# Small per-row operations moved to two-tensor VectorE forms, and the conversion of w2 staged over two steps

## The chip, the cores and the metric

The kernel runs on one core of a Trainium2 chip. The metric is the device time of one execution in microseconds; several executions are taken and the median is given. A profile of one further execution gives the trace from which durations are read. TensorE does the matrix products, VectorE (DVE in the profile), ScalarE (ACT) and GpSimd (POOL) do the elementwise work, and SyncE (SP) only issues DMAs.

## What is computed

```python
# q, k, v: (8, 8, 576, 64); tau = 0.02
scores = scale * np.matmul(q, k.transpose(0, 1, 3, 2))
thresh = np.max(scores, axis=-1, keepdims=True) - tau
scores = np.where(scores >= thresh, scores, -1000000000.0)
scores = scores - np.max(scores, axis=-1, keepdims=True)
attn = np.exp(scores)
attn = attn / (np.sum(attn, axis=-1, keepdims=True) + 1e-09)
x = np.matmul(attn, v)                    # heads side by side: (8, 576, 512)
...
mixed = np.real(np.fft.fft(np.fft.fft(x, axis=1), axis=2))
u = x + mixed
un = (u - mean(u)) / np.sqrt(var(u) + 1e-06)      # per row of 512
ch = np.maximum(un @ w_ch1, 0.0) @ w_ch2          # 512 -> 2048 -> 512
out = u + ch
```

Everything that the reference calls single precision is fp32 in the kernel. The weights w_ch1 and w_ch2 come as 64-bit floats, of which the kernel makes fp32 itself.

## The kernel before, in words

The eight batches have eight heads each, taken in pairs: 4 pairs a batch, 32 pairs in all. A pair has 5 row tiles (t = 0 to 4): four of 128 query rows for two heads, and a last one in which the 64 remaining rows of both heads share the 128 partitions. So there are 160 steps, i = 5 n + t.

A step's `scores(i)` makes the score rows in PSUM (L394, L405 for t = 4), takes each row's negated maximum on VectorE (`neg`, L416), makes the threshold of the row from it (`thr`, L420), takes the exponential on ScalarE (L426), and masks it on VectorE (L429), which also yields the row's sum `den`. A constant is added to the sum (L433), its reciprocal is taken (L436), and GpSimd copies it over 128 columns into `rec` (L438), because TensorE is to transpose it. For t = 4 GpSimd also copies 64 columns of the exponentials (L442). `transposed_weights(i - 1)`, one step later, turns exponentials and `rec` round on TensorE (L468, L469, L482) and ScalarE copies them out of PSUM. After a pair's five steps `weighted_values` makes v times the weights for both halves of the rows (L503), and VectorE multiplies each half by the turned reciprocals (`x`, L508). `fold_rows`, mostly on GpSimd (L531 to L544), and `mixing` make the Fourier part; its sums go to `u_t`, a ring of two batches' columns. `channels` then runs the two layers in groups of 384 rows: L685 for the first, L706 for the second.

The weights: `convert` turns one chunk of 64-bit floats into fp32 as a generator that stops between stages: a mask on VectorE (L283), a ScalarE scaling (L287), two VectorE operations (L289, L294), two ScalarE ones (L299, L303), and two GpSimd multiplies (L305, L306). There are 16 chunks of w_ch1 with stages in buffers of their own (loaded over SP's queue), and 16 of w_ch2, whose raw bits lie in the yet unused second half of `u_t`: two chunks' room, and loads on GpSimd's queue (L276). Matmuls that read `u_t` in the first half of the ring are ordered behind the conversion's writes, the last of which is L303. `center` takes the column mean from w_ch1, a group of 512 columns at a time; each has four subtractions (`less_mean`, L349), two on VectorE and two on GpSimd.

The order. Steps 0 to 19 (the first batch) are ordered wholly by hand: `step(i)` emits the scores, then one of the weighted values, a piece of centring (`later`), or two dummy matmuls that keep TensorE busy (`busy(2)`); then stages of two w_ch1 chunks around the previous step's transposed weights, then whatever centring has put into `after`. From step 20 on only TensorE's order is by hand; a scheduler orders the other engines. In each step there, `fill()` (three times) emits Fourier work and one or more matmul groups of `channels` within a budget. For the first sixteen steps from 21 on, one w_ch2 chunk is converted as a whole behind the step's reciprocal (`issue_after`, which fixes the order of issue on that engine alone), and the chunk two further on is then fetched:

```python
for _ in chunks.pop(0):
    pass
j = i - per_batch + 1
if j < NJ:
    chunks.append(w2_chunk(j))
```

Of the kernel before, what the change touches and what calls it, by code (L numbers as in the profile page):

```python
# [47 lines left out]
def kernel(  # L48
# [12 lines left out]
    nc = tc.nc  # L61
# [40 lines left out]
    def busy(n):  # L102

        for _ in range(n):
            pd = ps.tile([128, 4, 128], FP32, tag="mm", bufs=4, name="pd")
            four = bass.AP(
                tensor=ones.tensor, offset=ones.offset, ap=[list(ones.ap[0]), [0, 4], [1, 128]]
            )
            nc.tensor.matmul(pd[:, :, :], ones[:, :], four, start=True, stop=True)
# [76 lines left out]
    nc.vector.tensor_scalar(  # L186
        out=tau_pos[:], in0=tau_t[:], scalar1=0.0, scalar2=-1.0, op0=ALU.max, op1=ALU.mult
    )
    thr_off = const.tile([128, 1], FP32, name="thr_off")
    nc.vector.tensor_tensor(out=thr_off[:], in0=tau_pos[:], in1=below[:], op=ALU.add)  # L190

# [187 lines left out]
        if n + 1 < B * NPAIR:  # L381
            load_pair(n + 1)

    def scores(i):
        n, t = divmod(i, NT)
        qT, kT = heads[n][0:2]

        nh = 2 if t < 4 else 1
        sc = [ps.tile([128, 2, 512], FP32, tag="sc", name=f"sc{j}") for j in range(nh)]
        if t < 4:  # L390
            for c in range(2):
                for j in range(2):
                    hp = slice(64 * j, 64 * j + 64)
                    nc.tensor.matmul(  # L394
                        sc[j][:, c, 0:HALF], qT[hp, 128 * t : 128 * t + 128],
                        kT[hp, HALF * c : HALF * (c + 1)], start=True, stop=True,
                    )
        else:

            for j, c, c0, k0, w in (  # L400
                (0, 0, 0, 0, HALF), (1, 0, 0, 64, HALF), (0, 1, 0, HALF, HALF),
                (1, 1, 0, 64 + HALF, 512 - HALF), (1, 1, 512 - HALF, 0, 64),
            ):
                hp = slice(64 * j, 64 * j + 64)
                nc.tensor.matmul(  # L405
                    sc[0][hp, c, c0 : c0 + w], qT[hp, 512:S], kT[hp, k0 : k0 + w],
                    start=True, stop=True, skip_group_check=True,
                )
        neg = sb.tile([128, 2], FP32, tag="neg", bufs=3, name="neg")
        thr = sb.tile([128, 2], FP32, tag="thr", bufs=3, name="thr")  # L410
        den = sb.tile([128, 2], FP32, tag="den", bufs=3, name="den")


        e = sb.tile([128, 2 * S], FP32, tag="e", name="e")
        for j in range(nh):
            nc.vector.tensor_reduce(  # L416
                out=neg[:, j : j + 1], in_=sc[j][:, :, 0:HALF], axis=AXIS_XY, op=ALU.max,
                negate=True,
            )
        nc.vector.tensor_scalar(  # L420
            out=thr[:, 0:nh], in0=neg[:, 0:nh], scalar1=-1.0, scalar2=thr_off[:, :],
            op0=ALU.mult, op1=ALU.add,
        )
        for j in range(nh):
            ej = e[:, S * j : S * (j + 1)].rearrange("p (c n) -> p c n", c=2)
            nc.scalar.activation(  # L426
                out=ej, in_=sc[j][:, :, 0:HALF], func=ACT.Exp, bias=neg[:, j : j + 1], scale=1.0
            )
            nc.vector.scalar_tensor_tensor(  # L429
                out=ej, in0=sc[j][:, :, 0:HALF], scalar=thr[:, j : j + 1], in1=ej,  # L430
                op0=ALU.is_ge, op1=ALU.mult, accum_out=den[:, j : j + 1],
            )
        nc.vector.tensor_scalar(  # L433
            out=den[:, 0:nh], in0=den[:, 0:nh], scalar1=1e-9, scalar2=None, op0=ALU.add
        )
        behind[0] = nc.vector.reciprocal(den[:, 0:nh], den[:, 0:nh])  # L436
        rec = sb.tile([128, 2 * D], FP32, tag="rec", name="rec")
        nc.gpsimd.tensor_copy(  # L438
            rec[:, :].rearrange("p (j d) -> p j d", j=nh), _repeated(den[:, 0:nh], 2 * D // nh)
        )  # L440
        if t == 4:
            nc.gpsimd.tensor_copy(e[:, S : S + 64], e[:, 512:S])  # L442
        steps[i] = (e, rec)

    def transposed_weights(i):
# [307 lines left out]
    def step(i):  # L753

        n, t = divmod(i, NT)
        scores(i)
        if t == 1 and n > 0:
            weighted_values(n - 1)
            load_v(n + 1)
        elif later and later[0][0] <= i:  # L760
            later.pop(0)[1]()
        else:
            busy(2)
        if t == NT - 1:
            prep_pair(n + 1)
        for k in (i, i - 1):
            if k in chunks:
                next(chunks[k], None)
        if i > 0:
            transposed_weights(i - 1)  # L770
        for k in (i, i - 1):
            if k in chunks:
                next(chunks[k], None)
        while after:
            after.pop(0)()
        if i - 1 in chunks:
            next(chunks.pop(i - 1), None)
        if i > 0 and i + 3 < NCHUNK:
            chunks[i + 3] = w1_chunk(i + 3)
        if t == 3 and n > 0:  # L780
            fold_rows(n - 1)
# [5 lines left out]
    def center(g):  # L787
        def first():
            column_means(g)
            after.append(lambda: copy_mean(g))  # L790

        def second():
            mirrored(g)
            for c in range(ND):
                after.append(lambda c=c: less_mean(nc.vector if c % 2 else nc.gpsimd, g, c))

        later.append((ND * g + 6, first))
        later.append((ND * g + 7, second))
# [22 lines left out]
        later.pop(0)[1]()  # L821
    while after:
        after.pop(0)()
    chunks = [w2_chunk(j) for j in range(2)]
    by_hand.close()


# [1 line left out]
    for i in range(per_batch, total + 1):  # L829
        if i < total:  # L830
            scores(i)
        fill()
        n, t = divmod(i, NT)
        transposed_weights(i - 1)
        if t == 3 and n + 1 < B * NPAIR:
            prep_pair(n + 1)
        fill()
        if i > per_batch and chunks:
            with tc.issue_after(behind[0].ins):
                for _ in chunks.pop(0):  # L840
                    pass
            j = i - per_batch + 1
            if j < NJ:
                chunks.append(w2_chunk(j))
        fill()
        if t == 0:
            weighted_values(n - 1)
            fold_rows(n - 1)
            if n + 1 < B * NPAIR:
                load_v(n + 1)  # L850
        if i % per_batch == 0:
            b = i // per_batch - 1
            mixes.append(mixing(b))
            todo += MIX
            while (groups + 1) * GT <= (b + 1) * S:
                work.append((b, channels(groups)))
                groups += 1
                todo += GROUP
            keep = 0.4 * GROUP
            per_slot = (todo - spent - keep) / (3 * per_batch)  # L860
            budget = spent
# [49 lines left out]
```

## Time and profile before

| | |
|---|---|
| median of three runs | 1797.57 us (1796.34 to 1799.32) |
| the profiled execution's own time | 1798.21 us |
| its span, first to last instruction | 1796.1 us |
| mean granted TensorE clock | 0.984 |
| TensorE (PE) busy | 1728.0 us, 96% |
| VectorE (DVE) busy | 820.5 us, 46% |
| ScalarE (ACT) busy | 626.5 us, 35% |
| GpSimd (POOL) busy | 368.1 us, 20% |
| GpSimd's copies of 1/sum (L438) | 160, 50.2 us |
| GpSimd's copies for t = 4 (L442) | 32, 7.8 us |

The profile lists instructions by source line, engine and tile, with their number and mean time, and the idle time of the engine before them with the instruction that ended it ("<-"). A share of busy time is a mean over the whole span; since the work changes from the first batch to the later ones, tables by stage tell more. The clock is a share of TensorE's full speed.

### The profile page before, as it was taken

To read this page: it belongs to the slowest core of one execution; us is meant where nothing else is said; L and a number is where in the kernel's file an instruction comes from. 1 tells how busy PE (TensorE), PEld (TensorE's weight loads), DVE (VectorE), ACT (ScalarE), POOL (GpSimd) and SP (SyncE) were. 2 spreads that over 40 slices of the span, in tenths; PEclk is the share of its full clock that TensorE was granted. 3 is DMA by queue.
4 is the path that set the end of the run, shared out by engine and by line. 5 is a ranking of instruction groups with operands and counts; after the bars stand their busy time and mean duration, and the time that the engine had idled before them with its cause. 6 is when DMAs were issued, how large, how long until landed. Compare 5 with 4: busy or idle time off the path is not lost.

```text
span 1796.1 us, 21623 instructions
## 1 busy us (share of the span) xinstructions
PE 1728.0 (96%) x7872; PEld 995.9 (55%) x7872; DVE 820.5 (46%) x1985; ACT 626.5 (35%) x1270; POOL 368.1 (20%) x669
## 2 busy tenths in 40 slices
PE   8987787999999999999999999999999999999999
PEld 4545454556556656556556556555556565655453
DVE  7987574634334545544324545543434455521010
ACT  5654464334223334333224333432323333411010
POOL 5664564121110111112101031103011031110000
PEclk9989898999999999999999999999999999999999
DMA  5322122100010110100001110110001010000000
GB/s 153 106 57 68 55 73 67 33 26 20 7 38 14 26 33 14 34 26 20 13 26 27 26 27 20 27 32 14 14 26 27 19 27 20 1 12 6 12 6 18
DMA packets 130352, 57.03 MB, mean 32 GB/s; under 512 B 121123, under 2 KB 121125, under 8 KB 130246
## 3 DMA queue, kind: packets, MB, share of 16 engines
q1 hardware_dynamic: 126550, 46.96, 10.0%
q0 software_dynamic: 2304, 8.39, 1.4%
q8 instruction: 63, 1.03, 0.2%
q10 hardware_dynamic: 1392, 0.30, 0.1%
q14 instruction: 43, 0.35, 0.1%
HBM read 46.02 MB, written 9.44 MB: 31 GB/s over the span
## 4 chain that ended last, share of the span: by engine, by line
PE 86%; DVE 8%; ACT 3%; issue 1%; DMA 1%; SPq 1%; POOL 1%; ACTq 0%; DVEq 0%; POOLq 0%
PE ph L685 27%; PE po L706 27%; PE pv L503 9%; PE sc L394 7%; PE pw L482 6%; PE sc L405 2%; DVE e L429 2%; DVE neg L416 1%; PE py L594 1%; PE pa L611 1%; PE pe L468 1%; PE pn L669 1%; ACT e L426 1%; PE pa L615 1%; PE pe L469 1%
## 5 line engine op out<-in xcount | busy, mean ns | idle before, releaser
L685 PE MATMUL ph<-u_t,w 128*128 128x384 f32 x1536 | 531.8, 496 | 27.9 <-ACT u_t L303 27.1
L706 PE MATMUL po<-w,h 128*128 128x512 f32 x1152 | 524.2, 597 | 0.0
L685 PEld LDWEIGHTS ph<-u_t,w 128*128 128x128 f32 x1536 | 285.1, 192 | 220.0 <-ACT u_t L303 26.9
L426 ACT ACTIVATE e<-sc,neg 128x576 f32<-128x576 f32 x288 | 204.2, 738 | 487.0 <-DVE neg L416 485.6
L416 DVE TENSOR_REDUCE neg<-sc 128x1 f32<-128x576 f32 x288 | 205.8, 751 | 317.3 <-PE sc L394 226.8
L706 PEld LDWEIGHTS po<-w,h 128*128 128x128 f32 x1152 | 208.0, 190 | 222.0 <-issue 220.9
L429 DVE SCALAR_TENSOR_TENSOR e<-sc,thr,e 128x576 f32<-128x576 f32 x288 | 225.9, 815 | 39.2 <-ACT e L426 26.0
L438 POOL COPY rec<-den 128x128 f32<-128x128 f32 x160 | 50.2, 314 | 769.5 <-DVE den L436 443.1
L394 PE MATMUL sc<-kT,qT 64*128 64x288 f32 x1024 | 169.6, 442 | 5.3 <-DVE e L429 4.0
L482 PE MATMUL pw<-ident,e 128*128 128x128 f32 x1152 | 157.0, 276 | 10.8 <-DVE x L508 3.4
L691 ACT ACTIVATE h<-ph 128x384 f32<-128x384 f32 x96 | 47.0, 490 | 290.6 <-PE ph L685 290.6
L484 ACT COPY e_t<-pw 128x512 f32<-128x512 f32 x256 | 139.0, 592 | 7.4 <-PE pw L482 3.6
L394 PEld LDWEIGHTS sc<-kT,qT 64*128 64x128 f32 x1024 | 93.6, 192 | 85.4 <-issue 61.1
L482 PEld LDWEIGHTS pw<-ident,e 128*128 128x128 f32 x1152 | 132.7, 142 | 14.5 <-ACT tmp L626 4.1
L693 DVE TENSOR_SCALAR h<-ph 128x384 f32<-128x384 f32 x96 | 53.3, 555 | 184.1 <-PE ph L685 183.8
L508 DVE TENSOR_TENSOR x<-pv,ends 128x288 f32<-128x288 f32 x64 | 29.0, 455 | 172.4 <-PE pv L503 172.4
L472 ACT COPY ends<-pe 128x256 f32<-128x256 f32 x128 | 47.7, 373 | 138.0 <-PE pe L469 129.4
L713 DVE SCALAR_TENSOR_TENSOR u<-po,rstd,u 128x512 f32<-128x512 f32 x36 | 26.9, 748 | 132.4 <-PE po L706 132.4
L503 PE MATMUL pv<-e_t,v_in 128*64 128x288 f32 x512 | 68.3, 409 | 0.0
L503 PE MATMUL pv<-e_t,v_rev 128*64 128x288 f32 x512 | 68.3, 409 | 0.0
L420 DVE TENSOR_SCALAR thr<-neg,thr_off 128x2 f32<-128x2 f32 (+1 forms) x160 | 52.0, 325 | 5.2
L442 POOL COPY e<-e 128x64 f32<-128x64 f32 x32 | 7.8, 242 | 226.6 <-DVE e L429 163.3
(143 smaller groups left out, 1543.5 us busy)
## 6 DMA issues: line engine op xcount, KB each, us to landing
out_dram<-u SPq DMA_DIRECT2D x36, 256.0 KB, 2.0
qk_in<-in_q_dram SPq DMA_DIRECT2D x64, 128.0 KB, 2.4
stage<-in_moe_w_ch_dram SPq DMA_DIRECT2D x16, 512.0 KB, 4.2
v_in<-in_v_dram SPq DMA_DIRECT2D x64, 128.0 KB, 2.3
u_t<-in_moe_w_ch_dram POOLq DMA_DIRECT2D x16, 512.0 KB, 3.9
qk_in<-in_k_dram SPq DMA_DIRECT2D x31, 128.0 KB, 2.4
qk_in<-in_k_dram SPq DMA_DIRECT2D x31, 64.0 KB, 2.3
qk_in<-in_k_dram SPq DMA_DIRECT2D x93, 16.0 KB, 2.0
```

The lines of the kernel that those rows point to most:

```text
L394: nc.tensor.matmul(sc[j][:, c, 0:HALF], qT[hp, 128 * t : 128 * t + 128], kT[hp, HALF * c : HALF * (c + 1)], start=True, stop=True,)
L416: nc.vector.tensor_reduce(out=neg[:, j : j + 1], in_=sc[j][:, :, 0:HALF], axis=AXIS_XY, op=ALU.max, negate=True,)
L420: nc.vector.tensor_scalar(out=thr[:, 0:nh], in0=neg[:, 0:nh], scalar1=-1.0, scalar2=thr_off[:, :], op0=ALU.mult, op1=ALU.add,)
L426: nc.scalar.activation(out=ej, in_=sc[j][:, :, 0:HALF], func=ACT.Exp, bias=neg[:, j : j + 1], scale=1.0)
L429: nc.vector.scalar_tensor_tensor(out=ej, in0=sc[j][:, :, 0:HALF], scalar=thr[:, j : j + 1], in1=ej, op0=ALU.is_ge, op1=ALU.mult, accum_out ...
L438: nc.gpsimd.tensor_copy(rec[:, :].rearrange("p (j d) -> p j d", j=nh), _repeated(den[:, 0:nh], 2 * D // nh))
L482: nc.tensor.transpose(pw[:, c, :], e[:, c0 : c0 + 128], ident[:, :])
L484: nc.scalar.copy(e_t[:, 4 * j : 4 * j + 4, qs], pw[:, :, :])
L503: nc.tensor.matmul(pv[64 * j : 64 * j + 64, 0:HALF], vt[:, 2 * c + j, :], e_t[:, 4 * j + c, cols] if c < 4 else ends[:, 0, cols], start=(c ...
L685: nc.tensor.matmul(ph[:, 0:GT], w1[c][:, 128 * j : 128 * (j + 1)], u_t[:, c, c0 : c0 + GT], start=(c == 0), stop=(c == ND - 1),)
L693: nc.vector.tensor_relu(ht, ph[:, 0:GT])
L706: nc.tensor.matmul(po[:, :], hT[j // 4][:, j % 4, 128 * t : 128 * (t + 1)], w2[j][:, :], start=(j == 0), stop=(j == NJ - 1),)
```

## The change

Seven edits. The threshold and the addition to the sum become operations with two tensors (constants of two columns instead of a per-partition scalar and an immediate). The reciprocal is written over 128 columns by VectorE at once, reading each sum 64 or 128 times, and GpSimd's copy goes. The 64-column copy at t = 4 becomes a VectorE maximum of the columns with themselves. In the hand-ordered steps, `weighted_values` is emitted between the maskings of the step's first and second head. From step 16 on a single dummy matmul stands where there were two. At most two of the waiting centring pieces are emitted in a step, VectorE's two first. The conversion of a w_ch2 chunk is spread over two steps: mask and first scaling in one, the rest in the next, alternating with the next chunk's; a chunk is fetched when the one two before it is done, which is now a step before it is begun rather than two.

```diff
-    thr_off = const.tile([128, 1], FP32, name="thr_off")
-    nc.vector.tensor_tensor(out=thr_off[:], in0=tau_pos[:], in1=below[:], op=ALU.add)
+    thr_off = const.tile([128, 2], FP32, name="thr_off")
+    for j in range(2):
+        nc.vector.tensor_tensor(
+            out=thr_off[:, j : j + 1], in0=tau_pos[:], in1=below[:], op=ALU.add
+        )
+    least = const.tile([128, 2], FP32, name="least")
+    nc.vector.memset(least[:], 1e-9)
...
-    def scores(i):
+    def scores(i, between=None):
...
-        nc.vector.tensor_scalar(
-            out=thr[:, 0:nh], in0=neg[:, 0:nh], scalar1=-1.0, scalar2=thr_off[:, :],
+
+        nc.vector.scalar_tensor_tensor(
+            out=thr[:, 0:nh], in0=neg[:, 0:nh], scalar=-1.0, in1=thr_off[:, 0:nh],
             op0=ALU.mult, op1=ALU.add,
         )
...
-        nc.vector.tensor_scalar(
-            out=den[:, 0:nh], in0=den[:, 0:nh], scalar1=1e-9, scalar2=None, op0=ALU.add
-        )
-        behind[0] = nc.vector.reciprocal(den[:, 0:nh], den[:, 0:nh])
+            if between is not None:
+                between()
+                between = None
+        nc.vector.tensor_tensor(
+            out=den[:, 0:nh], in0=den[:, 0:nh], in1=least[:, 0:nh], op=ALU.add
+        )
         rec = sb.tile([128, 2 * D], FP32, tag="rec", name="rec")
-        nc.gpsimd.tensor_copy(
+        behind[0] = nc.vector.reciprocal(
             rec[:, :].rearrange("p (j d) -> p j d", j=nh), _repeated(den[:, 0:nh], 2 * D // nh)
         )
         if t == 4:
-            nc.gpsimd.tensor_copy(e[:, S : S + 64], e[:, 512:S])
+            last = e[:, 512:S]
+            behind[0] = nc.vector.tensor_tensor(out=e[:, S : S + 64], in0=last, in1=last, op=ALU.max)
...
-        scores(i)
         if t == 1 and n > 0:
-            weighted_values(n - 1)
+            scores(i, lambda: weighted_values(n - 1))
             load_v(n + 1)
+        else:
+            scores(i)
+        if t == 1 and n > 0:
+            pass
         elif later and later[0][0] <= i:
             later.pop(0)[1]()
         else:
-            busy(2)
+            busy(2 if i < NCHUNK else 1)
...
-        while after:
+        for _ in range(min(len(after), 2)):
             after.pop(0)()
...
-            for c in range(ND):
+            for c in (1, 3, 0, 2):
                 after.append(lambda c=c: less_mean(nc.vector if c % 2 else nc.gpsimd, g, c))
...
-    chunks = [w2_chunk(j) for j in range(2)]
+    chunks = {j: w2_chunk(j) for j in range(2)}
...
-        if i > per_batch and chunks:
+        j = i - per_batch - 1
+        if chunks and j >= 0:
+
             with tc.issue_after(behind[0].ins):
-                for _ in chunks.pop(0):
-                    pass
-            j = i - per_batch + 1
-            if j < NJ:
-                chunks.append(w2_chunk(j))
+                for _ in range(2):
+                    for m in (j, j - 1):
+                        if m in chunks:
+                            next(chunks[m], None)
+                if j - 1 in chunks:
+                    next(chunks.pop(j - 1), None)
+                    if j + 1 < NJ:
+                        chunks[j + 1] = w2_chunk(j + 1)
```

## The prediction

> **What bounds the kernel now.** I read the page first (engines, slices), then the busy table by stage, TensorE's waits, single lines, and the timeline around the longest wait. The table by stage, with cuts where the scores of step 0, step 20 and about step 37 begin:
>
> ```profile
> core 0: us, PE busy (x) PEld busy (x) DVE busy (x) ACT busy (x) POOL busy (x), PEclk, DMA share, GB/s
> 11.00:142.30 131.30, 112.21 (x578) 64.25 (x578) 111.56 (x240) 81.67 (x146) 84.16 (x129) 0.95 0.35 97
> 142.30:320.00 177.70, 139.85 (x719) 87.02 (x719) 109.94 (x249) 88.83 (x173) 86.36 (x111) 0.88 0.23 68
> 320.00:1796.10 1476.10, 1467.09 (x6556) 840.42 (x6554) 596.79 (x1487) 454.08 (x951) 195.03 (x412) 1.00 0.08 21
> ```
>
> Three stages. The last (320 on, 82% of the span) has TensorE busy 1467 of 1476 us at full clock; what VectorE or GpSimd gain there is worth nothing. The first, the 20 hand-ordered steps, has VectorE busy 85%. The middle, where w2 is converted, has TensorE idle for 38 us and a clock of 0.88. The change can only earn or lose in the first two. What TensorE waits for in the middle:
>
> ```profile
> PE ph L685 <- ACT u_t L303: 27.1, 9, 5.5
> PE py L594 <- DVE den L433: 4.9, 1, 4.9
> PE pw L482 <- ACT tmp L626: 2.8, 1, 2.8
> ```
>
> 27.1 us in nine waits are the layer-1 matmuls behind ScalarE's sign step (L303), which ends a w2 chunk's writes to u_t. The timeline of the longest:
>
> ```profile
> 182.09 0.90 DVE L283 TENSOR_SCALAR w<-u_t 128x512 int32<-128x512 int32 x1 [0.63 <-POOL u_t L637]
> 183.02 0.63 ACT L287 ACTIVATE w<-w 128x512 f32<-128x512 int32 x1 [1.57 <-DVE w L283]
> 183.68 1.05 DVE L289 SCALAR_TENSOR_TENSOR w<-u_t,w 128x512 f32<-128x512 uint32 x1 [0.70 <-ACT w L287]
> 184.15 1.13 POOL L637 TENSOR_TENSOR u_t<-x,tmp 1x287 f32<-1x287 f32 x1
> 184.77 0.80 DVE L294 TENSOR_SCALAR u_t<-u_t 128x512 int32<-128x512 int32 x1
> 185.65 0.74 ACT L299 ACTIVATE u_t<-u_t,shift 128x512 int32<-128x512 int32 x1 [2.00 <-DVE u_t L294]
> 186.30 0.65 ACT L303 ACTIVATE u_t<-u_t 128x512 f32<-128x512 int32 x1
> 187.10 1.62 PE L685 MATMUL ph<-u_t,w 128*128 128x384 f32 x2 [5.51 <-ACT u_t L303]
> ```
>
> The conversion runs VectorE, ScalarE, VectorE, ScalarE, each behind the other, and TensorE stands at the end. In 184.0 to 190.8 the busy table gives a granted clock of 0.50, so a wait is paid again in slow matmuls. For the first stage, the small VectorE rows:
>
> ```profile
> L420 DVE TENSOR_SCALAR thr<-neg,thr_off x160: 205/228/1511, 13.7 to 1568.4; 128x2 f32<-128x2 f32 x128, 128x1 f32<-128x1 f32 x32
> L294 DVE TENSOR_SCALAR stage<-stage x16: 428/434/1387, 22.7 to 124.9; 128x512 int32<-128x512 int32 x16
> L540 DVE TENSOR_TENSOR f<-x x8: 149/152/157, 153.3 to 1585.3; 128x2 f32<-128x2 f32 x8
> L289 DVE SCALAR_TENSOR_TENSOR w<-stage,w x16: 676/776/974, 21.9 to 124.2; 128x512 f32<-128x512 uint32 x16
> L289 DVE SCALAR_TENSOR_TENSOR w<-u_t,w x16: 657/693/1162, 161.3 to 316.9; 128x512 f32<-128x512 uint32 x16
> ```
>
> Minimum, median and maximum (ns): thr takes 0.23 us, or up to 1.5 us when GpSimd is busy.
>
> [...] thr reaches 1511 ns, and L289, which has two SBUF inputs, took 1.05 us at 183.68 instead of 0.69 while L633 and L637 ran. So two-tensor forms don't escape GpSimd's multiplies. [...]
>
> **The change part by part.** Durations are of the profiled execution: 1798.2 us with a span of 1796.1; the median of the three runs is 1797.6, 0.6 lower. The sum is made against 1798.2.
>
> First stage (20 steps, VectorE's time taken as on the path):
> - Thresholds: 228 (two heads) or 214 ns (one head, by-form row) to about 155: 16 x 0.073 + 4 x 0.06 = -1.4 us. The long cases stay, and a one-head threshold, free of them today, can now be caught; both ends are 0 and -4, since ScalarE's exponential often ends later anyway.
> - Sums: 165 (a 0.17 row at 83.91) to 153: -0.2.
> - 1/sum spread: the 163 ns reciprocal becomes one of 128 elements. [...] 20 x 0.131 = +2.6. The trace has no wide one; from 163 (two elements) to 169 (three, L702) at most 6 ns per element could be read, which I take as noise; half of it would give +7.6. Range 0 to +7.6. [...] Beyond stage 1 TensorE covers it.
> - The t = 4 copy of 64 elements on VectorE: by slope between L540 (152) and L535 (298 for 143) 216 ns, x 4 = +0.9. TensorE's one wait of 1.7 us for the GpSimd copy (L468 on L442) goes, but VectorE is next there: nothing counted.
> - GpSimd's rec copies (50.2 us in all) go. L289's median is 776 ns beside them in stage 1 and 693 in the middle: 16 x 0.08 = -1.3.
> - Centring: VectorE's two subtractions first, GpSimd's two a step later. L294 was caught by L349 three times (1387 against 434): -2.9; GpSimd's 3.1 us pair then meets the next step's rows, so I take half, -1.4 (0 to -2.9).
> - x between the maskings, steps 6, 11, 16. VectorE now stands at the second half of the weighted values with a mask, a sum and a reciprocal queued behind, for which the next scores' PSUM and the chunk wait. At step 11 the first mask ends at 83.1, x's second half was ready at 84.8; the order then ends 1.3 us later than now. Step 6 likewise some +0.9; at step 16 TensorE's 3.4 us wait for x shrinks by about 1.2. Sum +1.0 (-1.2 to +2.2).
> - One keep-warm matmul less at step 17: 2 of 48 records with 26.8 us, -1.1; half, -0.5, as VectorE is the bound nearby.
> Sum: -1.4 - 0.2 + 2.6 + 0.9 - 1.3 - 1.4 + 1.0 - 0.5 = -0.3 us.
>
> Middle stage:
> - Staging. From the reciprocal to the release now: 0.41 (L283) + 0.1 + 0.63 (L287) + 0.69 (L289) + 0.43 (L294) + 0.1 + 0.77 + 0.66 = 3.8 us. After: the new chunk's mask 0.41, then 0.69 + 0.43 of the old one, + 0.1 + 0.77 + 0.66 = 3.06: the ScalarE step leaves the path. Less 0.13 for the reciprocal: -0.6 at each of nine waits, -5.4. Which of a group's four matmuls waits alternates between the second and the fourth by chunk; the shift by one chunk swaps them and cancels.
> - Clock: the stage loses 0.12 x 177.7 = 21 us of clock; the waits shrink by 0.6 of a mean 3.0, a fifth[...]: -2.
> - The load's lead. Now chunk j+2 is fetched when j is done, two steps ahead; after it is one step ahead. In the built order the mask of chunk j stands straight ahead of chunk j-1's steps on VectorE in 13 of 15 cases. That closes a loop of one step: 0.41 + 0.69 + 0.43 + 0.1 + 0.77, then GpSimd 2 x 1.28, 0.3, and 3.9 to the landing = 9.2 us. L283's 16 rows now run from 160.1 to 315.8, 10.4 us each, so on the mean it fits, but steps of 5 to 6 us without a layer-1 wait (26, 31, 36) can't stay so short. VectorE then waits with the next scores' maximum queued behind it. Some of that takes the place of TensorE's waits a step later: +3 (0 to +14).
> - The last chunk ends a step later: +0.5.
> Sum: -5.4 - 2 + 3 + 0.5 = -3.9 us. Last stage: 0. In all -4.2: 1794.0 us.
>
> **The rivals.**
> - Nothing is left: the loop of 9.2 us eats the staging's gain (+3 becomes +6.5): 1797.5. For it: 10.4 is only 1.2 above the loop. Against: TensorE's waits are long.
> - Slower: the one-step lead decides. It does so once landings come later than VectorE's mask in most steps, not three, that is if steps would otherwise take under 9.2 us or GpSimd's fold rows stand ahead of the multiplies. Each such wait costs about 1 us, all 16 and one more step for halved clocks: +3 becomes +14, so 1805. A slow wide reciprocal (+4) adds to it. For it: the order puts the waiting mask ahead of the needed work. Against: VectorE was idle for 68 of the 178 us of that stage.
> - [...] thr's excess is (609 - 228) x 20 = 7.6 us in stage 1; two thirds hidden by the exponential, with a like part in the middle: -6 more, 1788. L289's 1.05 us speaks against it.
>
> **How the numbers follow.** A measurement tells about 0.2%, 3.6 us, from no change. Forecast case (1789 to 1794) 0.32, nothing left 0.25, slower 0.33[...]. Faster 0.42, same 0.25, slower 0.33. The likeliest's own range is 1788 to 1797; the whole one takes the slow case with its reciprocal and the lucky one: 1784 to 1808.
>
> **What would show it.** Right: the wait of ph for ScalarE's sign row falls from 27.1 to about 20 us, L283's successor rows stay about 10 us apart, the stage after 320 us is unchanged in length. The reciprocal's row shows 290 ns (a slope of its own would show 500 or more). Thresholds still show maxima over 1 us. Wrong: a DMA as releaser of the mask row for tens of us, a stage clock below 0.88, or VectorE idle before x at steps 6 and 11 for more than 2 us.

## The result and the profile after

The changed kernel takes 1815.55 us (median of four runs, 1812.72 to 1820.17) against 1796.95 for the kernel before in the same session; the ratio is 1.0105, with a 95% interval of 1.0081 to 1.0130. It is slower by about 19 us, where 4 us less were forecast; the forecast's whole range ended at 1808. The profiled span is 1813.7 us (before: 1796.1), at the same mean clock of 0.984.

The table by stage with the cuts that the prediction used, for the changed kernel:

```profile
11.00:142.30 131.30, 109.95 (x541) 62.40 (x542) 120.45 (x234) 78.96 (x141) 75.08 (x104) 0.95 0.36 97
142.30:320.00 177.70, 131.90 (x677) 82.08 (x677) 114.28 (x240) 84.69 (x163) 68.46 (x75) 0.88 0.21 62
320.00:1813.00 1493.00, 1480.44 (x6636) 848.65 (x6632) 694.41 (x1534) 463.87 (x965) 164.37 (x279) 1.00 0.08 21
```

VectorE (the third pair of numbers) is busy 120.45 of 131.3 us in the first stage (it was 111.56), and yet fewer matmuls fit (541, were 578). With fixed cuts the work slides from one row into the next, so the stages are better cut at each kernel's own steps 20 and 40. First the middle row of the kernel before, cut in that way:

```profile
142.30:333.10 190.80, 152.12 (x779) 93.92 (x778) 118.89 (x271) 96.29 (x186) 88.51 (x114) 0.88 0.23 66
```

Then the three rows of the changed kernel:

```profile
11.00:149.60 138.60, 115.95 (x576) 66.10 (x576) 125.93 (x247) 82.22 (x147) 79.15 (x108) 0.95 0.34 93
149.60:348.80 199.20, 151.50 (x779) 93.39 (x778) 131.17 (x272) 97.53 (x186) 77.63 (x88) 0.89 0.22 63
348.80:1813.60 1464.80, 1454.84 (x6496) 833.63 (x6495) 672.03 (x1490) 447.77 (x936) 151.13 (x262) 1.00 0.08 21
```

The same 779 matmuls stand in both middle rows, so lengths compare: 138.6 against 131.3 in stage 1 (+7.3), 199.2 against 190.8 in the middle (+8.4), and 1464.8 against 1462.9 after that (+1.9). In the middle, idle being the length less the busy time, TensorE was busy 0.6 us less and idle 9.0 us more. From the groups by line of the changed kernel, with forms kept apart (count, busy us, mean ns, idle before):

```profile
L446 DVE RECIPROCAL rec<-den 128x128 f32<-128x128 f32 x160 | 152.0, 950 | 3.9
L711 DVE RECIPROCAL rstd<-rstd 128x3 f32<-128x3 f32 x12 | 2.0, 169 | 2.9 <-ACT rstd L708 2.9
L426 DVE SCALAR_TENSOR_TENSOR thr<-neg,thr_off 128x2 f32<-128x2 f32 x128 | 36.6, 286 | 3.9
```

The wide reciprocal takes 950 ns where 294 were taken for it, an estimate of 1.04 ns for each of 126 elements more than the two that take 163. In the trace before, VectorE's two-tensor rows have such a slope (152 ns for 2 elements, 298 for 143); no reciprocal row shows it. For the reciprocal, from 3 to 128 elements, it is (950 - 169) / 125 = 6.25 ns an element: the 6 ns that the prediction read off and put aside as noise. The two-head thresholds fell from a mean of 353 ns to 286. The forecast went by the median, which was to fall from 228 ns to about 155; over all thresholds it fell to 160. But the twenty of stage 1, where this was to count, take 12.54 us together where they took 12.19. TensorE's waits in the changed kernel (us in total, times, longest):

```profile
PE ph L694 <- ACT u_t L308: 30.2, 9, 8.6
PE sc L399 <- DVE e L435: 6.5, 6, 2.2
```

The wait that was to fall from 27.1 to about 20 us rose to 30.2, with a longest one of 8.6 us where it was 5.5. (L694 and L308 are L685 and L303 of the kernel before.)

### The profile page after: what moved, and what is told of

It reads as the page before. It is cut to its first block, busy times and chain, and to the rows that moved or that the text cites. A ratio compares the mean times of both kernels' runs of the same rounds, so it can differ in the third digit from the quotient of the medians.

```text
span 1813.7 us, 21328 instructions
## 1 busy us (share of the span) xinstructions
PE 1731.3 (95%) x7870; PEld 997.3 (55%) x7870; DVE 931.3 (51%) x2019; ACT 629.3 (35%) x1270; POOL 310.3 (17%) x477
## 4 chain that ended last, share of the span: by engine, by line
PE 82%; DVE 9%; issue 3%; ACT 2%; POOL 2%; DMA 1%; SPq 0%; DVEq 0%; POOLq 0%; ACTq 0%
PE ph L694 27%; PE po L715 27%; PE pv L512 8%; PE sc L399 7%; PE pw L491 5%; DVE e L435 2%; DVE neg L421 2%; PE sc L410 2%; DVE rec L446 1%; PE py L603 1%; ACT e L432 1%; PE pa L620 1%; PE pn L678 1%; PE pa L624 1%; PE pe L477 1%
## 5 line engine op out<-in xcount | busy, mean ns | idle before, releaser
L694 PE MATMUL ph<-u_t,w 128*128 128x384 f32 x1536 | 531.9, 495 | 33.7 <-ACT u_t L308 30.2
L694 PEld LDWEIGHTS ph<-u_t,w 128*128 128x128 f32 x1536 | 284.7, 192 | 227.1 <-ACT u_t L308 36.2
L446 DVE RECIPROCAL rec<-den 128x128 f32<-128x128 f32 x160 | 152.0, 950 | 3.9
L540 POOL TENSOR_TENSOR half<-x 128x287 f32<-128x287 f32 x48 | 38.2, 816 | 561.4 <-DMA x<-swap 310.5
L642 POOL TENSOR_TENSOR u_t<-x,tmp 128x289 f32<-128x289 f32 (+1 forms) x48 | 35.0, 740 | 577.6 <-DVE tmp L639 553.7
L517 DVE TENSOR_TENSOR x<-pv,ends 128x288 f32<-128x288 f32 x64 | 29.1, 456 | 157.5 <-PE pv L512 157.4
```

Source lines behind the costliest of these rows:

```text
L446: behind[0] = nc.vector.reciprocal(rec[:, :].rearrange("p (j d) -> p j d", j=nh), _repeated(den[:, 0:nh], 2 * D // nh))
L694: nc.tensor.matmul(ph[:, 0:GT], w1[c][:, 128 * j : 128 * (j + 1)], u_t[:, c, c0 : c0 + GT], start=(c == 0), stop=(c == ND - 1),)
```

## The experiments

**The theories.** Theory: the wide reciprocal is the cause, through VectorE's chain, and staging gives back a part. Rival: the staging is the cause, because a chunk's load now leads by one step. Each was put on the kernel before alone and taken out of the changed kernel alone; then the smaller edits were tried, and last the question of what covers what in the middle stage.

All ratios are against the kernel before on the same chip in the same session:

| kernel | median us | ratio (95%) |
|---|---|---|
| before + wide reciprocal | 1819.67 | 1.0123 (1.0109 to 1.0137) |
| before + staging | 1801.30 | 1.0024 (1.0014 to 1.0034) |
| changed, narrow reciprocal and GpSimd copy | 1801.02 | 1.0024 (1.0014 to 1.0034) |
| changed, no staging | 1819.50 | 1.0126 (1.0112 to 1.0140) |
| before + staging, sign step first | 1793.36 | 0.9966 (0.9952 to 0.9979) |
| before + two-tensor forms | 1798.80 | 1.0001 (0.9992 to 1.0011) |
| before + x between the maskings | 1798.24 | 1.0002 (0.9992 to 1.0011) |
| before + centring | 1795.44 | 0.9992 (0.9982 to 1.0001) |
| before + row blocks apart | 1768.57 | 0.9827 (0.9813 to 0.9840) |
| the same + wide reciprocal | 1790.29 | 0.9959 (0.9945 to 0.9973) |
| the same + staging, sign step first | 1777.00 | 0.9895 (0.9880 to 0.9910) |
| the same, both small copies on VectorE | 1778.83 | 0.9897 (0.9884 to 0.9911) |
| changed + row blocks apart | 1804.79 | 1.0043 (1.0030 to 1.0057) |

Kernels that are set against each other below ran in part on different chips, so besides the medians the ratios are compared. Lengths of stages come from one profile of each kernel. How far such lengths repeat can be seen where the work is the same: stage 1 is the same in the kernel before and in the four that only convert w2 in another way (staging alone, sign step first, row blocks apart, row blocks apart and staging), and it took 127.5 to 131.6 us; the middle is the same in the kernel before, with x between and with centring, and it took 188.4 to 191.3. Differences of such a size between two profiles show nothing.

### The reciprocal

The wide reciprocal on the kernel before, nothing else:

```diff
-        behind[0] = nc.vector.reciprocal(den[:, 0:nh], den[:, 0:nh])
         rec = sb.tile([128, 2 * D], FP32, tag="rec", name="rec")
-        nc.gpsimd.tensor_copy(
+        behind[0] = nc.vector.reciprocal(
             rec[:, :].rearrange("p (j d) -> p j d", j=nh), _repeated(den[:, 0:nh], 2 * D // nh)
         )
```

> The kernel before, with 1/sum spread over 128 columns by VectorE's reciprocal as the only edit. Theory 1: 1812 to 1820 us, since 0.79 us more on VectorE in each of some 36 steps lies on the path for about half to two thirds. Theory 2: at most +9 us, 1806 or less, all of it before step 20.

Measured: 1819.67 us, ratio 1.0123, which is 22 us on 1797.6, as the first theory said. This one edit costs about as much as the whole change, if not more. The row of this kernel, and its first two stages cut at its own steps 20 and 40:

```profile
L437 DVE RECIPROCAL rec<-den 128x128 f32<-128x128 f32 x160 | 152.1, 951 | 4.7
```

```profile
11.00:153.70 142.70, 118.68 (x578) 66.09 (x578) 125.85 (x244) 82.05 (x147) 77.21 (x108) 0.92 0.33 89
153.70:355.40 201.70, 158.60 (x779) 97.51 (x778) 129.86 (x270) 96.71 (x186) 80.55 (x94) 0.85 0.22 63
```

Stage 1 is 11.4 us longer (142.7 against 131.3). VectorE is busy there 14.3 us more (125.85 against 111.56; twenty steps by 951 - 163 ns are 15.8), of which only 2.9 found room in its idle time. The middle is 10.9 us longer (201.7 against 190.8), and that in two ways: TensorE is idle 4.4 us more, and the same 779 matmuls are busy 6.5 us more at a granted clock of 0.85 instead of 0.88. That the longer waits bring about the slower matmuls fits what the trace before has at its longest wait (a granted clock of 0.50 in 184.0 to 190.8; two layer-1 matmuls took 0.81 us ahead of the wait, the six behind it 4.04), but this run does not show it apart. The last stage grew by 1.7 us. (The three make 24 us; the profiled execution, 1822.21 us, was the slowest of the four.)

The changed kernel with the narrow reciprocal and GpSimd's copy put back:

```diff
-        behind[0] = nc.vector.reciprocal(
+        behind[0] = nc.vector.reciprocal(den[:, 0:nh], den[:, 0:nh])
+        nc.gpsimd.tensor_copy(
             rec[:, :].rearrange("p (j d) -> p j d", j=nh), _repeated(den[:, 0:nh], 2 * D // nh)
         )
```

> The changed kernel, with 1/sum taken over two columns again and spread by GpSimd, all other edits kept. Theory 1 (the wide reciprocal, 950 ns a piece, is the whole loss): stage 1 and the middle come back, 1792 to 1797 us. Theory 2 (the one-step lead of the w2 loads costs the middle stage its 8 us): stage 1 comes back, the middle stays late, 1804 to 1808 us.

Measured: 1801.02 us, ratio 1.0024, between the ranges of the two theories. All but 4 us of the change's loss is gone: the reciprocal is most of it, not the whole.

Whether reading one value 64 or 128 times is what takes the time, and not the division, was tested by letting VectorE copy the repeated values instead (on the kernel with the row blocks apart, explained below; the copy of the exponentials at t = 4 moved with it):

```diff
         behind[0] = nc.vector.reciprocal(den[:, 0:nh], den[:, 0:nh])
...
-        nc.gpsimd.tensor_copy(
+        behind[0] = nc.vector.tensor_copy(
             rec[:, :].rearrange("p (j d) -> p j d", j=nh), _repeated(den[:, 0:nh], 2 * D // nh)
         )
         if t == 4:
-            nc.gpsimd.tensor_copy(e[:, S : S + 64], e[:, 512:S])
+            behind[0] = nc.vector.tensor_copy(e[:, S : S + 64], e[:, 512:S])
```

> The kernel before with the row blocks written apart, the reciprocal narrow, and both small copies (the spread of 1/sum over 128 columns and the 64 columns of the exponentials at t = 4) by VectorE copies in place of GpSimd's. Theory, it is the reciprocal that costs some 6 ns an element, and not reading one value many times over: the copy of 128 repeated values takes 100 to 300 ns, the waits on GpSimd's rec and e copies (5.2 and 4.4 us in the run with rows apart) go, the VectorE chain of stage 1 becomes 20 x 0.1 to 0.3 = 2 to 6 us longer, so 1763 to 1772 us. Rival, it is the repeated reading: the copy takes 700 ns or more and the time is 1780 us or more.

The rows of that kernel:

```profile
L444 DVE COPY rec<-den 128x128 f32<-128x128 f32 x160 | 43.5, 272 | 4.6
L443 DVE RECIPROCAL den<-den 128x2 f32<-128x2 f32 x128 | 20.9, 164 | 3.6
```

The copy of the same repeated values takes 272 ns where the wide reciprocal takes 950, so it is the division. But the time was outside the expected range: 1778.83 us, 10 above the kernel it was built on. The 20 spreads by 0.272 and the 4 copies by 0.295 us add 6.6 us to VectorE in stage 1, and stage 1 takes 138.3 us here against 131.3 in the kernel before; the waits on GpSimd's two copies are gone from the table, but their time was not gained. Here, moving small work onto the engine that sets the pace lost, though each piece was short.

### The staging

The staging alone on the kernel before (its diff is that of the change):

> The kernel before, with the staging of w2 over two steps as the only edit. Theory 1: 1793 to 1799 us; the release of TensorE's waits comes 0.7 us earlier and the shorter lead costs about as much. Theory 2: 1803 to 1808 us, with VectorE's mask row waiting for the load.

Measured: 1801.30 us, ratio 1.0024, between the ranges of the two theories: a loss of 4 us where 3.9 were to be gained. Its waits on the sign row, and its middle stage:

```profile
PE ph L685 <- ACT u_t L303: 22.5, 7, 7.8
```

```profile
142.60:339.20 196.60, 155.50 (x779) 95.73 (x778) 118.36 (x271) 96.53 (x186) 88.71 (x114) 0.85 0.22 64
```

The waits fell from 27.1 to 22.5 us, as they were meant to: six make 14.7, and one alone 7.8. The stage is 5.8 us longer all the same (196.6 against 190.8), 3.4 of it in longer busy time at a clock of 0.85 instead of 0.88. By the starts of each step's scores in the two traces, this kernel is 0.8 us behind the kernel before at step 32, 9.5 us at step 33, and 4.7 us at step 34, because in step 33 the kernel before has the longer wait (3.62 us, against 1.63 here). So 3.9 us of the long wait remain. The timeline of this kernel in between:

```profile
269.12 0.67 DVE L289 SCALAR_TENSOR_TENSOR w<-u_t,w 128x512 f32<-128x512 uint32 x1
269.81 1.27 POOL L306 TENSOR_TENSOR w<-w,u_t 128x512 f32<-128x512 f32 x1
269.89 2.90 DVE L294 TENSOR_SCALAR u_t<-u_t 128x512 int32<-128x512 int32 x1
271.04 1.46 POOL L555 TENSOR_TENSOR sums<-f 128x608 f32<-128x608 f32 x1
272.45 0.78 POOL L276 DMA_DIRECT2D u_t<-in_moe_w_ch_dram  x1
272.82 0.76 ACT L299 ACTIVATE u_t<-u_t,shift 128x512 int32<-128x512 int32 x1 [3.20 <-DVE u_t L294]
...
276.42 0.43 DVE L283 TENSOR_SCALAR w<-u_t 128x512 int32<-128x512 int32 x1 [3.63 <-DMA u_t<-in_moe_w_ch_dram]
276.88 0.63 ACT L287 ACTIVATE w<-w 128x512 f32<-128x512 int32 x1 [3.30 <-DVE w L283]
277.42 0.63 ACT L303 ACTIVATE u_t<-u_t 128x512 f32<-128x512 int32 x1
...
278.11 4.21 PE L685 MATMUL ph<-u_t,w 128*128 128x384 f32 x6 [7.75 <-ACT u_t L303]
```

Read from the end: TensorE waits for the old chunk's sign step (L303). On ScalarE that step stands behind the new chunk's scaling (L287), which waits for its mask (L283), which waits for the new chunk's load, which GpSimd issued only at 272.45, behind a multiply and a folding operation (L306, L555). So in this kernel the load's lead of one step, which the prediction had as a cost on VectorE, reaches the very wait that staging was to shorten through ScalarE, where the two chunks alternate. The exponent step L294, 2.90 us instead of the usual 0.43, adds to it: it ends 0.3 us after the second of GpSimd's L306 and L555, two operations in a row. The six matmuls that follow take 4.21 us.

If that order is the link, it can be cut by issuing the older chunk first in each half (this turns the order on VectorE too):

```diff
-                    for m in (j, j - 1):
+                    for m in (j - 1, j):
```

> The kernel before with the w2 staging alone, but in each step the older chunk's operations are issued ahead of the newer one's, so that on ScalarE the sign step no longer stands behind the scaling of the newer chunk, which waits for that chunk's load. Theory, the wait of 7.8 us of ph at step 32 in the run with the staging alone is the load, issued one step ahead on GpSimd's queue behind the folding, and it reaches ph only through that order on ScalarE: the wait falls to 4 us or less and the time from 1801.3 to 1796 to 1798 us. Rival, the conversion is late at step 32 whatever the order (GpSimd is busy with the folding for 9 us, and the exponent step took 2.9 us beside it): the wait stays above 6 us and the time at 1800 to 1802 us.

The same place in this kernel, and its row of waits:

```profile
268.29 0.78 POOL L276 DMA_DIRECT2D u_t<-in_moe_w_ch_dram  x1
268.66 0.76 ACT L299 ACTIVATE u_t<-u_t,shift 128x512 int32<-128x512 int32 x1 [3.20 <-DVE u_t L294]
...
269.31 0.66 ACT L303 ACTIVATE u_t<-u_t 128x512 f32<-128x512 int32 x1
...
270.01 4.21 PE L685 MATMUL ph<-u_t,w 128*128 128x384 f32 x6 [4.56 <-ACT u_t L303]
...
272.18 1.51 DVE L283 TENSOR_SCALAR w<-u_t 128x512 int32<-128x512 int32 x1 [3.55 <-DMA u_t<-in_moe_w_ch_dram]
```

```profile
PE ph L685 <- ACT u_t L303: 18.3, 6, 4.7
```

Measured: 1793.36 us, below the range of its theory; ratio 0.9966, about 6 us less than before (4 to 9 by the interval) and 8 to 10 less than the staging in the change's order. The load is as late as it was, but the sign step no longer waits for it. The wait there fell to 4.6 us, not quite to the 4 expected, for L294 still takes 2.90 us. That one wait is not the whole gain: by the starts of the steps this kernel is 3.5 us ahead of the staging in the change's order at step 32, 8.2 at step 34 and 9.9 at step 40, so step 32 makes about half of it. Where the order gives the rest was not traced.

The changed kernel without its staging:

> The changed kernel, with w2 converted a chunk a step and fetched two ahead as before. Theory 1: 1811 to 1819 us, as the wide reciprocal is still there. Theory 2: 1806 to 1809 us, the middle stage's 8 us come back.

Measured: 1819.50 us, just above the range of the first theory; ratio 1.0126 (1.0112 to 1.0140) against 1.0105 (1.0081 to 1.0130) for the whole change. The medians differ by 4 us, but the intervals overlap, so a gain by the staging beside the wide reciprocal is not shown. The profiles show none either: the kernel without staging is 9.5 us behind the kernel before at step 20 and 18.6 at step 40, the changed one 7.3 and 15.7. So 2.2 of the 2.9 us between them stand there before the conversion of w2 begins, where the two kernels do the same.

Within the middle the two lose their time in different places. Between steps 20 and 32 the kernel without staging falls back to 14.7 us, the changed one only to 9.1; in step 32 the changed one loses 8.1 us, of which 3.1 remain at step 34, to its longest wait. Its timeline there:

```profile
278.89 0.77 POOL L281 DMA_DIRECT2D u_t<-in_moe_w_ch_dram  x1
...
282.85 0.43 DVE L288 TENSOR_SCALAR w<-u_t 128x512 int32<-128x512 int32 x1 [2.91 <-DMA u_t<-in_moe_w_ch_dram]
283.19 0.68 DVE L294 SCALAR_TENSOR_TENSOR w<-u_t,w 128x512 f32<-128x512 uint32 x1
...
283.98 0.43 DVE L299 TENSOR_SCALAR u_t<-u_t 128x512 int32<-128x512 int32 x1
284.44 0.74 ACT L304 ACTIVATE u_t<-u_t,shift 128x512 int32<-128x512 int32 x1 [0.50 <-DVE u_t L299]
285.09 0.64 ACT L308 ACTIVATE u_t<-u_t 128x512 f32<-128x512 int32 x1
...
285.79 4.21 PE L694 MATMUL ph<-u_t,w 128*128 128x384 f32 x6 [8.55 <-ACT u_t L308]
```

The late load is the cause here too, but by another way than in the kernel with staging alone. VectorE stands 2.91 us at the new chunk's mask (L288), and the old chunk's two operations (L294, L299) come behind it in VectorE's order; behind them follow ScalarE's two steps and the release. In the changed kernel it is thus VectorE's order, and not ScalarE's, that puts the load ahead of the sign step.

### The small edits

The two-tensor forms alone (thresholds and sums), the weighted values between the maskings alone, and the centring alone, each as in the change:

> The kernel before with the two-tensor forms of the threshold and of the sum alone (no other edit). The profile of the changed kernel has the threshold row at 286 ns (353 before) and the row of the sum at 211 ns (196). Theory, these two are worth what their rows say in the twenty steps of stage 1: 20 x (67 - 15) ns = 1.0 us, so 1796.5 us and the same two durations. Rival, the loss of 2 us by step 20 that the run with the narrow reciprocal shows against the run with the staging alone comes from here: step 20 starts 2 us late and the time is 1799 us or more.

> The kernel before with x between the maskings alone (weighted_values called between the two masking operations at t = 1). Theory of the prediction: +1.0 us in stage 1 (1798 us), range -1.2 to +2.2. If this edit is what makes the run with the narrow reciprocal 2 us late between steps 5 and 10, step 7 starts some 2 us late here and step 10 too, and the time is 1799 us; if not, step 10 starts within 0.7 us of the kernel before and the time is 1796 to 1798 us.

> The kernel before with the centring alone changed (at most two of its four subtractions in a step, in the order 1, 3, 0, 2). The prediction had it at -1.4 us: 1796.5 us. By what the other parts have shown (all edits but the wide reciprocal and the staging together move the time by less than 0.5 us against the staging alone), it is nothing: 1797 to 1799 us.

Measured: 1798.80, 1798.24 and 1795.44 us beside 1797.95, 1797.95 and 1797.85 for the kernel before. None can be told from nothing. In the first the median of all thresholds fell from 228 to 161 ns, but the twenty of stage 1 took 12.17 us together where they took 12.19. Ten of these took 0.64 us or more before the change, each beside a GpSimd operation (the mean of the twenty was 609 ns), and the sum stayed. Step 20 of it starts 0.5 us late, not the 2 of the rival. Step 10 of the second starts 2.0 us late and step 20 only 0.7. The third is 0.9992 (0.9982 to 1.0001): the forecast -1.4 us lies in the interval, and so does zero. The copy at t = 4 and the keep-warm matmul were not tried alone; with all small edits in, the changed kernel with the narrow reciprocal has the same ratio as the staging alone (1.0024), so together they are within some 2.5 us of nothing; and beside the wide reciprocal too, for the changed kernel without staging (1.0126) is where the wide reciprocal alone is (1.0123).

### What lies under the reciprocal in the middle stage

The failed step said that TensorE covers the wide reciprocal beyond stage 1. One way in which it could reach TensorE is the wait on the sign row, since a chunk is converted behind the reciprocal. That wait can be taken away: the matmuls read columns 0 to 383 of a row block of u_t, the conversion writes columns 576 on of two blocks in one operation, so no element is shared, and only the span from the first to the last address of the write takes in the second block's first columns. If the order of the matmuls behind the write goes by that span, then written one block at a time there is nothing to wait for (in the last two places of the diff the new lines stand for one operation over both blocks; only w2 is converted in this way):

```diff
-        queue.dma_start(out=raw, in_=src.bitcast(INT32).rearrange("p (c n) -> p c n", c=2))
+        words = src.bitcast(INT32).rearrange("p (c n) -> p c n", c=2)
+        parts = [slice(0, 1), slice(1, 2)] if apart else [slice(0, 2)]
+        for s in parts:
+            queue.dma_start(out=raw[:, s, :], in_=words[:, s, :])
...
+        for s in parts:
+            nc.vector.tensor_scalar(
+                out=low[:, s], in0=high[:, s], scalar1=20, scalar2=0x7FF,
+                op0=ALU.logical_shift_right, op1=ALU.bitwise_and,
+            )
...
+        for s in parts:
+            nc.scalar.activation(
+                out=low[:, s], in_=low[:, s], func=ACT.Relu, bias=shift[:, :],
+                scale=float(1 << 23),
+            )
+            nc.scalar.activation(out=sign[:, s], in_=high[:, s], func=ACT.Sign)
```

> The kernel before, with the conversion of a w2 chunk writing u_t one row block at a time (the load, the exponent step on VectorE, and both ScalarE steps are each issued twice, 512 columns of one block each time, in place of once over two blocks). Nothing else changes, but no layer-1 matmul is ordered behind those writes any more. Theory, the 27.1 us of waits of ph on the sign row are TensorE time that nothing else needs, as are the spells of half clock that follow them: most of 27 us is gained, 1770 to 1785 us, and the waits table has no ph <- u_t row. Rival, the score chain on VectorE and ScalarE is late as well and takes the place of that wait: ph's waits are gone but others rise by as much, 1793 to 1797 us. [...]

Measured: 1768.57 us, just under the range of its theory; ratio 0.9827: 31 us less by the ratio (29 between the medians), the fastest kernel of the study. TensorE's longest waits in it, and its middle stage from its step 20 to its step 40:

```profile
PE pe L475 <- POOL rec L444: 5.2, 3, 2.2
PE sc L411 <- DVE e L435: 5.1, 2, 2.8
PE py L600 <- DVE den L439: 4.9, 1, 4.9
```

```profile
138.50:300.20 161.70, 139.00 (x780) 88.30 (x778) 124.33 (x287) 99.71 (x218) 95.67 (x130) 0.96 0.27 78
```

The row of ph behind the sign step (27.1 us before) is gone, as it must be if the order goes by the span, and no wait of its size took its place. The middle is 29.1 us shorter (161.7 against 190.8): idle time fell from 38.7 to 22.7, and TensorE's busy time by 13.1, at a clock of 0.96 instead of 0.88. The theory of that run holds, its rival falls. (The profiled execution, 1765.01 us, was the fastest of four, and its stage 1, where nothing was changed, is 3.8 us shorter than in the kernel before. What is set against this profile below looks that much too dear, or a part of it.)

The whole change on top of it, the wide reciprocal alone on top of it, and the staging alone (older chunk first) on top of it:

> The changed kernel, whole, with the conversion of a w2 chunk writing u_t one row block at a time, so that no layer-1 matmul waits for the sign row. Theory, the 11 us that the wide reciprocal costs in the middle stage reach TensorE through that wait (the conversion is issued behind the reciprocal), and the 11 us of stage 1 through the score chain itself: the first go, the second stay. Against the same edit on the kernel before (1768.6 us) that is +11 for stage 1, +1.9 for the three later mixings and about 1 for the rest: 1780 to 1784 us. Rival, in the middle stage too the score chain itself carries the 0.8 us of each step: the whole 18.6 us between the two kernels stay, 1786 to 1790 us.

> The kernel before with the row blocks written apart and the wide VectorE reciprocal, and no staging. Open is how the 36 us that the whole change cost on the kernel with rows apart (1768.6 to 1804.8) divide: the staging alone cost 8.4 of them. Theory, in the middle stage nothing covers the wide reciprocal once the wait of ph is gone, it lies on the score chain at its full 0.79 us in each of 20 steps: +11.4 in stage 1, +15 in the middle, +1.9 later, 1796 to 1800 us. Rival, TensorE's work in the middle does cover it when VectorE isn't held by late loads, and the 36 us are the load's lead made worse by the reciprocal: +11.4 and +1.9 with 0 to 5 between, 1781 to 1787 us.

> The kernel before with the row blocks written apart and the w2 chunks staged over two steps, the older chunk issued first. Theory, staging moved the time only through the waits of ph on the sign row, which are gone: the same as rows apart alone, 1766 to 1771 us. Rival, the shorter stretches of conversion on VectorE and ScalarE also let the score chain through sooner: 1760 to 1765 us; or the load a step ahead keeps its cost on VectorE and the chain: 1772 to 1776 us.

Measured: 1804.79, 1790.29 and 1777.00 us, against 1768.57; both cases expected of the first two missed, and the third lies just above the highest of its cases. The middle stages of the three, in that order:

```profile
149.60:335.90 186.30, 152.47 (x780) 93.27 (x778) 134.34 (x289) 99.27 (x218) 82.92 (x103) 0.89 0.23 67
```

```profile
151.70:323.60 171.90, 146.57 (x780) 91.36 (x779) 135.25 (x286) 100.01 (x218) 86.85 (x110) 0.90 0.26 74
```

```profile
140.90:310.30 169.40, 145.92 (x779) 92.71 (x778) 120.60 (x287) 99.49 (x218) 96.92 (x130) 0.91 0.26 75
```

With the wide reciprocal alone the middle grew by 10.2 us (171.9 against 161.7), about as much as on the kernel before (10.9). The medians say the same: the two kernels differ by 21.7 us, which less 11.4 for stage 1 and 1.6 later leaves 8.7. So it does not come through the wait for the sign row, which is not there; nor does all of 20 x 0.79 us come through. Of the 10.2 us only 2.6 are idle time; 7.6 are longer busy time at a clock of 0.90 instead of 0.96. Staging, with nothing left to release, costs 7.7 us in the middle, 6.9 of it in busy time. Both together in the whole change (with the small edits, and the staging in the change's order) cost 24.6 us, where the sum is 17.9. Whether they make each other worse is open: in the whole times the excess is 6 us by the medians and 3 by the ratios, where each kernel's ratio is known to about 2.5 us, and the order of the chunks alone, worth 8 to 10 us on the kernel before, may be what makes it. With the rows apart the change's order was not run alone. The trace shows one place where late loads and the rest of VectorE's work meet. The row of VectorE's waits in the changed kernel with rows apart, and a stretch of its timeline:

```profile
DVE w L291 <- DMA u_t<-in_moe_w_ch_dram: 25.6, 11, 3.7
```

```profile
243.43 0.43 DVE L291 TENSOR_SCALAR w<-u_t 128x512 int32<-128x512 int32 x1 [3.11 <-DMA u_t<-in_moe_w_ch_dram]
243.78 0.49 DVE L303 TENSOR_SCALAR u_t<-u_t 128x256 int32<-128x256 int32 x2
...
244.18 0.15 DVE L432 SCALAR_TENSOR_TENSOR thr<-neg,thr_off 128x1 f32<-128x1 f32 x1
...
244.85 0.80 DVE L441 SCALAR_TENSOR_TENSOR e<-sc,thr,e 128x576 f32<-128x576 f32 x1
...
245.71 1.80 PE L405 MATMUL sc<-kT,qT 64*128 64x288 f32 x5 [2.03 <-DVE e L441]
```

VectorE stands 3.11 us at the mask of a chunk whose load has not landed, with the next threshold and masking behind it, for which TensorE then waits. That is the mechanism of the prediction's slow rival; in the kernel with staging and no wide reciprocal the same waits are 15.8 us in 8 places.

## Why the prediction was wrong, step by step

**1/sum spread, +2.6 us: the step that failed, in size and in place.** The size: 950 ns, not 294; at 6.25 ns an element the term for stage 1 is 20 x 0.787 = 15.7, of which 11.4 was measured. The slope was in the prediction, read from 163 and 169 ns, and put aside for 1.04 ns an element, an estimate of the author's that no row of a reciprocal showed; even the range's end (+7.6) was made with half of the slope. The place: "Beyond stage 1 TensorE covers it" was wrong for the middle stage, which grew by 10.9 us (10.2 without the sign row's wait), and right for the last, where the 120 steps from step 40 on cost 1.7 us together. In the middle TensorE had idle time (38.7 us of 190.8 before) and a lower clock (0.88), and more work on VectorE was not covered there.

**Staging, -5.4 and -2 us, with +3 for the load's lead: a second step that failed.** The release did come, where the order let it: with the older chunk first the waits on the sign row are 18.3 us of 27.1, where about 20 were expected, and the kernel gains some 6 us, where the sum said 3.9. The -2 for the clock was the author's estimate. The load's lead was seen, with 9.2 us for its loop, GpSimd's folding ahead of it as the condition, and the new chunk's mask ahead of the old chunk's steps on VectorE. But its cost was put on the next scores' maximum, at about 1 us for each wait. That the old chunk's release stands behind the same load, on VectorE in the changed kernel and on ScalarE in the one with staging alone, is not in its sum. In the changed kernel the mask row waits for loads 6.7 us in 4 places, not the tens of us that were to show this case; one of them stood ahead of a wait of TensorE of 8.55 us. The staging alone lost 4 us; the order alone is worth 8 to 10.

**Thresholds and sums, -1.6.** The size was right for a threshold without GpSimd work beside it, as most are: the median threshold fell from 228 to 160 ns (155 expected). The place was wrong: in stage 1, where it was to count, they took 609 ns on the mean before the change and 627 after. The fourth case, given 0.10, was that these forms are free of the long times beside GpSimd. It is refuted by the same numbers and by a longest threshold of 1.41 us: in either kernel 25 thresholds took over 0.40 us, each of them beside a GpSimd operation, and of those without one none took more than 0.23 us before and 0.16 after. One-head thresholds, at most 0.22 us before, took up to 0.55. The sums rose from a mean of 196 to 211 ns, with a median of 160.

**x between, +1.0, and centring, -1.4.** Neither can be told from nothing. VectorE's idle time before x in the changed kernel's hand-ordered steps was one wait of 0.3 us, so the idle time of more than 2 us that was feared at steps 6 and 11 did not come.

**Copies, L289, keep-warm: +0.9, -1.3, -0.5.** The 64-column maximum took 233 ns (216 estimated), and the two-tensor step on w1 chunks fell from 778 to 701 ns, as estimated. No run shows any of it in the time.

**Last stage, 0.** It grew by 1.9 us, 0.6 at each of the three later mixings, where matmuls now wait 5.8 us in all for ScalarE and VectorE (4.0 before).

**The rivals.** The slower case had the right sign, and both its mechanisms are in the traces: late loads with the next scores behind them, and a slow reciprocal. It put 4 us on the reciprocal, which by itself costs 22; that its middle value, 1805, lies nearer to the result than the forecast is in part luck. What stays open is the clock: with the row blocks apart it makes most of what the reciprocal and the staging cost in the middle stage, and one profile of each kernel does not tell which wait sets off which loss of it.

## What to carry to other kernels

Take the time of an operation at a size that no row shows from the slope of the same operation, however small the two sizes are, and keep the full slope as the range's end. Two such small sizes can mislead (one and two elements showed no slope at all, 164 and 163 ns), so where the term is large, a run of that one edit is the better answer. Before work is put down as covered, ask of the stage in which it lies whether the covering engine is ever idle there: where it is, a longer chain behind it cost idle time here (4.4 us in the middle stage with the wide reciprocal alone), and came with a lower clock (0.85 in place of 0.88). Where a wait is to be shortened, follow its releaser back over every queue that it stands in, and ask first whether the order behind the wait is needed at all: here two writes in place of one took away 27 us of it.

## What the runs showed of the hardware

- VectorE's fp32 reciprocal took 163 or 164 ns for one or two elements per partition in the kernel before, 169 for three, and 950 for 128 in the changed one: 6.25 ns an element from three to 128. A VectorE copy of the same 128 repeated values took 272 ns.
- A VectorE operation on one tensor of 0.43 us (L294) took 2.90 beside two GpSimd operations that followed each other, and ended 0.3 us after the second (the kernel with the staging alone).
- With the row blocks apart, TensorE's idle time in the middle stage was 22.7 us instead of 38.7 and the granted clock 0.96 instead of 0.88; the same matmuls were busy 13.1 us less.
